# Two feed-forward layers behind chunked attention: other buffers and another order where the second layer begins, and one sum reordered in the last pass

## The chip, the cores and the metric

The kernel runs on one core of one Trainium2 chip. The metric is device time in microseconds (us); one number is the median of three runs. The engines are called as in the profile: PE is TensorE (matmul), PEld its weight load, DVE is VectorE, ACT is ScalarE, POOL is GpSimd, and SP is SyncE, whose one queue (SPq) issues every transfer of this kernel in program order.

## What is computed

```python
def reference(**kwargs):                      # batch 8, heads 8, seq 576, head_dim 64
    attn_out = _attn_ref(q, k, v)             # softmax attention inside chunks of 64
    x = attn_out.transpose(0, 2, 1, 3).reshape(B * S, H * D)      # 4608 tokens x 512
    g = x @ w_gate                            # 512 -> 1536
    x = silu(g) * (x @ w_val) @ w_out         # layer 1: 1536 -> 512
    h = x @ w_in                              # 512 -> 2048
    return h * sigmoid(1.702 * h) @ w_out2    # layer 2: 2048 -> 512
```

Everything is float32. Each number is split into a high part that PE multiplies exactly (fp32r) and a low remainder, and a product is three matmuls (high*high, high*low, low*high: lines 249, 250 and 251).

## The kernel before

**Tiling.** The 4608 tokens are nine blocks of 512 (`b` = 0 to 8). The program makes four passes over the blocks, two for layer 1 (`p` = 0, 1) and two for layer 2 (`p` = 2, 3). A pass holds a part of the hidden width in SBUF; in layer 2 a pass has two groups of four times 128 hidden columns. Products of 2x2 blocks are made with seven multiplications in place of eight (Strassen and Winograd), so everything comes in sevens, under the labels "1" to "7".

**One layer-2 group** is `group_gated` (line 632). Its seven input products (`product`, 12 matmuls of 128 columns by 256 tokens each) go through PSUM. As a rule all seven share one bank, `ga`: some labels add on top of the former one, others start the bank anew, and between two products ACT or DVE reads the bank out (`follow`, line 660, into the tiles `u` and `c`). Such a product cannot start before the bank was read. Where `early` is set, labels "2", "3" and "4" have the banks `gb`, `s` and `a` for themselves, and the order is "1263745". From the four finished quarters, `gate` (line 647) makes h * sigmoid(1.702 h): a Sigmoid on ACT (line 651 in the profile) and a multiply on DVE. The four results stand in one tile of the ring `xr`, which has one buffer only. DVE then adds them up to the seven combinations, and `parts` (line 656) splits each into high (a cast on ACT) and low (a subtraction on DVE or POOL). The homes of the parts are the buffers of `HOMES` (line 629): `hh`, `hl`, `h`, `q`, `k`, `v`, `xt`.

**The second product** of a group is 14 `last_product`s (line 714), two per label in the order "1245673", each 6 matmuls. They add over the two groups of a pass into seven half banks: "1" and "2" in `ya`, "4" and "5" in `yb`, "6", "7", "3" in `gb`, `s`, `a` (`o_banks`, line 726). After the second group `o_sum` (line 732) reads them out; in pass 2 it stores partial sums to DRAM, in pass 3 it adds the stored ones and writes the output. The last products of one group are interleaved with the input products of the next (`put`, line 874).

**Where the layers meet.** At the end of pass 1 `block_sum` (line 795) finishes the layer-1 output of a block in a tile of `xr`; `x_to_dram` (line 556) forms seven token combinations (`token_combos`: four subtractions, three of them into the three buffers of `xt`), splits each by ACT plus DVE or POOL, and stores both halves to DRAM, where layer 2 loads them. For the last block the seven splits take seven different pairs of buffers.

**Weights.** The weights of the next pass are converted during a pass (`group_to_dram`, line 403): loads into the ring `raw`, four ACT instructions and four DVE instructions per tile (lines 328 to 337), sums `st`, a cast and a subtraction on POOL into `ws`, a store. Each pair of tiles is a job; `spread` (line 848) gives the eight jobs of pass 2 a due time each. A job takes two tiles of the ring `t` and two loads of two half tiles, so four Sigmoid-sized ACT instructions of line 328.

**What sets the order.** All instructions are recorded as `op`s with an estimated cost, a priority (`prio`, a due time in us; lower is first) and their dependences. `Program.emit` (line 99) then writes each engine's queue: it always takes the op that can start earliest by these estimates, and the priority decides only between ops that can start within 0.1 us (DVE) or 0.3 us (the others) of each other. For layer 2, hand-overs between ACT, DVE and POOL are planned at 1.0 us (`prog.slack`). The order is fixed before the kernel runs.

**Names used below.** G0 and G1 are the two groups of pass 2, block 0, so the first two groups of layer 2; H0 is the first group of block 1. Before, only G0 has `early`.

```python
alone = {"2": "gb", "3": "s", "4": "a"} if early else {}
z = ring["ga"].new([P, 2, HT])
bank = {label: ring[alone[label]].new([P, 2, HT]) if label in alone else z for label in ORDER[2]}
for i, label in enumerate("1263745" if early else ORDER[2]):
```

Of the kernel before, what the change touches and what calls it, by code (L numbers as in the profile page):

```python
# [13 lines left out]
ALU = mybir.AluOpType  # L14
# [4 lines left out]
P = 128  # L19
# [122 lines left out]
def attention_two_moe_kernel(ctx: ExitStack, tc: tile.TileContext, q, k, v, wg, wv, wo, wi, wo2, out):  # L142
# [36 lines left out]
    HT = BT // 2  # L179
    NB = NT // BT  # L180
# [77 lines left out]
    for layer, nf, per in ((1, NF1, 6), (2, NF2, 8)):  # L258
        for f0 in range(0, nf, per):
            gs = []  # L260
            for j in range(0, per, 2 * layer):
                g = Group()
# [199 lines left out]
    xr = {}  # L462
# [93 lines left out]
    def x_to_dram(xb, b, prio):  # L556
        for n, (m, src, cut) in enumerate(token_combos(xb, prio)):
            i = ORDER[2].index(m)
            pairs = ["qk", "ve"] if b < NB - 1 else ["qk", "ve", "tt", ("raw", "raw"), ("ws", "ws"), "hh", "te"]
            hi, lo = [ring[t].new([P, 2, HT], F32R) for t in pairs[n % len(pairs)]]  # L560
            split(hi, lo, src, 512, prio + n, "pool" if b < NB - 1 else ("dve", "pool")[n % 2], cut)
            for c, s in enumerate((hi, lo)):
                store(x_dram[1][:, b, i, c * 512:(c + 1) * 512], Buf(lambda s=s: s.ap.rearrange("p a t -> p (a t)"), None, None, s), [xd[1][b][i].part(None)], prio + n + 2)
# [65 lines left out]
    HOMES = {"1": ("hh", "hl"), "2": ("hh", "hl"), "4": ("hh", "hl"), "5": ("h", "h"), "6": ("q", "k"), "7": ("v", "xt"),  # L629
             "3": ("xt", "xt")}  # L630

    def group_gated(g, xs, at, put, early):


        s1, u2, u3 = [ring["u"].new([P, 2, HT]) for _ in range(3)]
        made = {}
        hs = []

        quarters = []

        def quarter():
            if not quarters:
                c = ring["c"].new([P, 2, 2, HT])
                quarters.extend(c.part(lambda ap, k=k: ap[:, k]) for k in range(2))
            return quarters.pop(0)

        def gate(c, k, prio):
            if not hs:
                hs.append(ring["xr"].new([P, 4, 2, HT]))
            h = hs[0].part(lambda ap: ap[:, k])  # L650
            op("act", act_us(512), lambda: nc.scalar.activation(out=h.ap, in_=c.ap, func=AF.Sigmoid, scale=1.702),  # L651
               [c], [h], prio, "sig")
            tt(h, h, c, ALU.mult, 512, prio)
            return h

        def parts(label, src, prio, eng="dve"):
            made[label] = [ring[t].new([P, 2, HT], F32R) for t in HOMES[label]]
            split(*made[label], src, 512, prio, eng)

        def follow(label, prio):  # L660
            m = bank[label]
            if label == "1":
                copy(s1, m, 512, prio, near=0.3)
            elif label == "6":
                copy(u2, m, 512, prio, near=0.3)
            elif label == "7":
                copy(u3, m, 512, prio, near=0.3)
                tt(u2, u2, u3, ALU.subtract, 512, prio, "pool")
            elif label == "5":
                c = quarter()  # L670
                copy(c, m, 512, prio, near=0.3)
                tt(u2, u2, c, ALU.add, 512, prio, "pool")
                a["22"] = gate(c, 3, prio + 1)
                parts("4", a["22"], prio + 3, "pool")
            elif label == "2":
                c = quarter()
                tt(c, s1, m, ALU.add, 512, prio, near=0.3)
                a["11"] = gate(c, 0, prio + 1)
                parts("1", a["11"], prio + 2)
            elif label == "4":  # L680
                c = quarter()
                tt(c, u3, m, ALU.subtract, 512, prio, near=0.3)
                a["12"] = gate(c, 1, prio + 1)
                parts("2", a["12"], prio + 3)
            else:
                c = quarter()
                tt(c, u2, m, ALU.add, 512, prio, near=0.3)
                a["21"] = gate(c, 2, prio + 1)

        a = {}  # L690
# [4 lines that stand above are left out]
            n = ORDER[2].index(label)  # L695
            product(bank[label], W[g][n], xs[n], label in "675", at(i), 0.25)
            if label != "3" or not early:
                follow(label, at(i))
            if i == 6:
                if early:  # L700
                    follow("3", at(i))
                prio = at(i)
                tt(a["22"], a["21"], a["22"], ALU.add, 512, prio + 1)
                parts("5", a["22"], prio + 2)
                tt(a["21"], a["11"], a["21"], ALU.subtract, 512, prio + 2)
                tt(a["11"], a["22"], a["11"], ALU.subtract, 512, prio + 2)
                parts("6", a["11"], prio + 3)
                parts("7", a["21"], prio + 4)
                tt(a["12"], a["12"], a["11"], ALU.subtract, 512, prio + 4)
                parts("3", a["12"], prio + 5)  # L710
            put(i)
        return made
# [19 lines left out]
    def o_sum(p, b, label, banks, kept, prio):  # L732

        final = p == NPASS - 1

        def part_of(k, tag):

            t = ring[tag].new([P, 2, 256])
            if final:
                load(t.part(lambda ap: ap.rearrange("p a c -> p (a c)")), o_dram[:, b, k], prio - 14, [od2[b, k]])  # L740
            return t

        def out_quarter(k, t):
            if final:
                t0 = b * BT + (k // 2) * HT
                dst = out[t0:t0 + HT, k % 2 * 256:k % 2 * 256 + 256].rearrange("(t p) c -> p t c", p=P)
                store(dst, t, [], prio)
            else:
                od2[b, k] = Buf(None)
                store(o_dram[:, b, k], Buf(lambda: t.ap.rearrange("p a c -> p (a c)"), None, None, t), [od2[b, k]], prio)  # L750

        m = banks[label]
        if label == "1":
            kept["s"] = ring["e"].new([P, 2, 256])
            copy(kept["s"], m, 512, prio)
        elif label == "2":
            c = part_of(0, "yv")
            if final:
                tt(c, c, kept["s"], ALU.add, 512, prio, "pool")
                tt(c, c, m, ALU.add, 512, prio)  # L760
            else:
                tt(c, kept["s"], m, ALU.add, 512, prio)
            out_quarter(0, c)
        elif label == "6":
            tt(kept["s"], kept["s"], m, ALU.add, 512, prio)
        elif label == "7":
            u2, u3 = kept["s"], ring["e"].new([P, 2, 256])
            tt(u3, u2, m, ALU.add, 512, prio)
            c = part_of(3, "yv")
            if final:  # L770
                tt(c, c, u3, ALU.add, 512, prio, "pool")
                tt(c, c, banks["5"], ALU.add, 512, prio)
            else:
                tt(c, u3, banks["5"], ALU.add, 512, prio)
            out_quarter(3, c)
            c = part_of(2, "t") if final else u3
            if final:
                tt(c, c, u3, ALU.add, 512, prio, "pool")
            tt(u2, u2, banks["5"], ALU.add, 512, prio)
            tt(c, c, banks["4"], ALU.subtract, 512, prio)  # L780
            out_quarter(2, c)
            if final:
                kept["c"] = part_of(1, "t")
                tt(kept["c"], kept["c"], u2, ALU.add, 512, prio, "pool")
        elif label == "3":
            u4 = kept["c" if final else "s"]
            tt(u4, u4, m, ALU.add, 512, prio)
            out_quarter(1, u4)
# [6 lines left out]
    def block_sum(p, b, ys, e, prio):  # L795
# [10 lines left out]
            xr[b] = ring["xr"].new([P, KD, BT])  # L806
        tt(xr[b].part(lambda ap: ap[:, e]), s, ys[e], ALU.add, 512, prio)
        if e == KD - 1:
            x_to_dram(xr.pop(b), b, prio + 3)


    op("pool", 0.6, lambda: make_identity(nc, ident.ap), [], [ident], -99)
# [14 lines left out]
    early = [((g.name, var, i), g.pairs[var][i]) for g in gs0[:2] for var in range(2) for i in range(2)]  # L827
# [3 lines left out]
    for u in range(UPB):  # L831
        bufs = None
        if u:
            ve = ring["c"].new([P, 2, 512])
# [13 lines left out]
    def spread(p):  # L848

        if p + 1 >= NPASS:  # L850
            return []
        jobs = [j for g in passes[p + 1][1] for j in group_to_dram(g, 0)]
        a = start[p][0] + (100 if p == 0 else 10)
        z = start[p + 1][0] - 60
        return [(a + (z - a) * i / len(jobs), j) for i, j in enumerate(jobs)]

# [6 lines left out]
    for p, (layer, gs) in enumerate(passes):  # L863
        jobs = spread(p)
        for b in range(NB):
            t = start[p][b]
            xs = X.pop((p, b))
            for j, g in enumerate(gs):
# [30 lines left out]
                            pend.append(fn)  # L899
                else:  # L900
                    prog.slack = 1.0
                    parts = group_gated(g, xs, at, put, after_first)
                    if j == 0:
                        banks, kept = {}, {}
                    ws = {}
# [84 lines left out]
```

## Time and profile before

| | us |
|---|---|
| median of 3 runs (lowest, highest) | 1790.44 (1789.31, 1791.83) |
| the profiled execution, its own time | 1790.32 |
| its span, first to last instruction | 1788.5 |
| PE busy in it | 1711.5 (96%) |
| DVE / ACT / POOL busy | 1310.8 / 876.9 / 761.6 |

The profiled execution stands 1.8 us above its span (start and end of the program) and 0.1 us below the median. Pass 2 begins on PE at about 1014 us of the span, pass 3 at about 1398 us. Busy time of PE has to be read with the count of matmuls beside it: at half clock a matmul counts as busy for longer, and matmuls overlap.

### The profile page before, as it was taken

What the parts mean: (1) busy time and instruction counts of PE and PEld (TensorE: products, weight loads), DVE (VectorE), ACT (ScalarE), POOL (GpSimd) and SP (SyncE); (2) the same over time, 40 slices, a digit from 0 to 9 for tenths busy, and PEclk for the clock granted to TensorE, in tenths of its full rate; (3) what the DMA queues carried; (4) which work ended last, traced back from release to release, by engine and by line L of the source; (5) the groups of instructions that cost most, each with busy time, mean ns of one, the idle gap of its engine ahead of it and who ended that gap; (6) DMA issues with size and microseconds to landing.
All of it is one profiled execution on the core that took longest, in us unless ns stands there. A gap on an engine that the chain in (4) does not pass through costs nothing.

```text
span 1788.5 us, 36703 instructions
## 1 busy us (share of the span) xinstructions
PE 1711.5 (96%) x14392; PEld 1623.6 (91%) x14392; DVE 1310.8 (73%) x1884; ACT 876.9 (49%) x1534; POOL 761.6 (43%) x762
## 2 busy tenths in 40 slices
PE   6779999999999999999999978999999999999997
PEld 6769988989899999999999968999999999999997
DVE  6887788778876477655555679888877677777777
ACT  6766665666563344333333354555544444444442
POOL 5664455455632145412222247556651233334333
PEclk8889999999999999999999998999999999999999
DMA  7468887788768989877778988788888977666664
GB/s 254 167 217 271 270 298 239 253 297 285 245 236 329 339 288 314 284 260 247 251 246 304 367 323 280 266 277 286 290 279 304 360 262 237 232 213 224 225 220 152
DMA packets 187325, 477.93 MB, mean 267 GB/s; under 512 B 20112, under 2 KB 47760, under 8 KB 187152
## 3 DMA queue, kind: packets, MB, share of 16 engines
q1 hardware_dynamic: 187152, 475.58, 77.6%
q8 instruction: 114, 1.87, 0.4%
q14 instruction: 59, 0.48, 0.1%
HBM read 334.46 MB, written 141.03 MB: 266 GB/s over the span
## 4 chain that ended last, share of the span: by engine, by line
PE 75%; DVE 15%; issue 3%; DMA 1%; ACT 1%; POOL 0%; POOLq 0%; SPq 0%; DVEq 0%; ACTq 0%
PE ga L249 9%; PE ga L251 9%; PE ga L250 9%; PE yb L249 4%; PE ya L250 4%; PE ya L251 4%; PE ya L249 4%; PE yb L251 4%; PE yb L250 4%; PE gb L249 4%; PE gb L251 4%; PE gb L250 4%; DVE xr L242 3%; PE s L249 2%; PE s L251 2%
## 5 line engine op out<-in xcount | busy, mean ns | idle before, releaser
L249 PE MATMUL ga<-x,w 128*128 128x256 f32 x1652 | 477.1, 289 | 28.8 <-DVE c L242 12.1
L250 PE MATMUL ga<-x,w 128*128 128x256 f32 x1652 | 468.6, 284 | 3.0 <-DVE x L242 3.0
L251 PE MATMUL ga<-x,w 128*128 128x256 f32 x1652 | 468.7, 284 | 0.1
L249 PEld LDWEIGHTS ga<-x,w 128*128 128x128 f32 x1652 | 314.8, 191 | 43.4 <-DVE c L242 18.2
L250 PEld LDWEIGHTS ga<-x,w 128*128 128x128 f32 x1652 | 314.9, 191 | 7.6 <-DVE x L242 3.3
L251 PEld LDWEIGHTS ga<-x,w 128*128 128x128 f32 x1652 | 314.8, 191 | 0.3 <-POOL w L242 0.3
L233 ACT COPY u<-ga 128x512 f32<-128x512 f32 x231 | 135.1, 585 | 254.6 <-PE ga L251 249.8
L242 DVE TENSOR_TENSOR c<-u,ga 128x512 f32<-128x512 f32 x146 | 99.8, 684 | 138.4 <-PE ga L251 137.1
L242 DVE TENSOR_TENSOR h<-h,c 128x512 f32<-128x512 f32 x216 | 170.6, 807 | 10.0 <-ACT h L613 8.4
L651 ACT ACTIVATE xr<-c 128x512 f32<-128x512 f32 x144 | 90.0, 631 | 162.4 <-DVE c L242 118.1
L249 PE MATMUL gb<-x,w 128*128 128x256 f32 x496 | 143.0, 288 | 2.4 <-DVE c L242 2.4
L251 PE MATMUL gb<-x,w 128*128 128x256 f32 x496 | 141.4, 285 | 0.0
L250 PE MATMUL gb<-x,w 128*128 128x256 f32 x496 | 141.1, 284 | 0.0
L242 POOL TENSOR_TENSOR u<-u 128x512 f32<-128x512 f32 x36 | 53.7, 1492 | 191.7 <-ACT u L233 191.7
L242 DVE TENSOR_TENSOR c<-u,gb 128x512 f32<-128x512 f32 x124 | 84.6, 682 | 67.4 <-ACT u L233 42.3
L613 ACT ACTIVATE h<-c 128x512 f32<-128x512 f32 x108 | 68.1, 633 | 120.5 <-DVE c L242 120.2
L242 DVE TENSOR_TENSOR xr<-xr,c 128x512 f32<-128x512 f32 x144 | 115.7, 809 | 14.2 <-ACT xr L651 14.2
L242 DVE TENSOR_TENSOR xr<-xr 128x512 f32<-128x512 f32 x144 | 118.1, 820 | 1.4
L235 POOL CAST ws<-t 128x256 fp32r<-128x256 f32 x78 | 45.3, 581 | 172.3 <-DMA od_b<-ws 81.3
L242 POOL TENSOR_TENSOR k<-xr,q 128x512 fp32r<-128x512 f32 x24 | 42.3, 1762 | 158.3 <-DVE xt L242 63.9
L249 PEld LDWEIGHTS gb<-x,w 128*128 128x128 f32 x496 | 95.2, 192 | 5.6 <-DVE c L242 3.0
L235 POOL CAST ws<-st 128x256 fp32r<-128x256 f32 x88 | 48.4, 549 | 121.2 <-DMA od_b<-ws 54.0
(239 smaller groups left out, 5179.2 us busy)
## 6 DMA issues: line engine op xcount, KB each, us to landing
x<-x_dram SPq DMA_DIRECT2D x189, 512.0 KB, 5.5
o<-od_b SPq DMA_DIRECT2D x126, 512.0 KB, 4.5
o<-od_a SPq DMA_DIRECT2D x102, 512.0 KB, 5.2
x_dram<-x SPq DMA_DIRECT2D x63, 512.0 KB, 4.7
wd_b<-ws SPq DMA_DIRECT2D x56, 256.0 KB, 4.8
od_b<-ws SPq DMA_DIRECT2D x56, 256.0 KB, 5.2
w<-wd_b SPq DMA_DIRECT2D x28, 512.0 KB, 6.8
raw<-in_moe_w_out SPq DMA_DIRECT2D x56, 255.8 KB, 5.1
```

What stands on the lines that cost most here:

```text
L233: op("act", act_us(n), lambda: nc.scalar.copy(out=dst.ap, in_=cut(src.ap)), [src], [dst], prio, near=near)
L235: op("pool", pool_us(0.6 * n), lambda: nc.gpsimd.tensor_copy(dst.ap, cut(src.ap)), [src], [dst], prio)
L242: lambda: e.tensor_tensor(out=dst.ap, in0=of_a(a.ap), in1=of_b(b.ap), op=by), [a, b], [dst], prio, near=near)
L249: nc.tensor.matmul(o, ah, bh, start=first, stop=False, **kind)
L250: nc.tensor.matmul(o, ah, bl, start=False, stop=False, **kind)
L251: nc.tensor.matmul(o, al, bh, start=False, stop=last, **kind)
L613: op("act", act_us(512), lambda h=h, i=i: nc.scalar.activation(out=h.ap, in_=of(0)(c[i].ap), func=AF.Sigmoid), [c[i]], [h], prio, "sig")
L651: op("act", act_us(512), lambda: nc.scalar.activation(out=h.ap, in_=c.ap, func=AF.Sigmoid, scale=1.702), [c], [h], prio, "sig")
```

## The change

1. `x_to_dram` for the last block splits through two pairs of buffers, (`raw`, `raw`) and (`ws`, `ws`), in turn, in place of seven pairs; a pair is free again when both its stores have landed. Its sums and splits get a priority 5 us later.
2. G0's gates (`apart`) write to three tiles of `t` and one of `e` in place of the one tile of `xr`.
3. G1 gets `early`: the banks `gb`, `s`, `a` and the order "1263745".
4. The conversion jobs of pass 2 are due from 70 us after the start of the pass, before 10; their last due time stays.
5. `o_sum` of pass 3: before, POOL added quarter 2's partial sum to u3 and DVE then subtracted bank "4"; now DVE subtracts bank "4" from u3 in place first, and POOL adds the result to the stored sum last. In pass 2 the same instructions come in the same order.

```diff
@@ x_to_dram
-            pairs = ["qk", "ve"] if b < NB - 1 else ["qk", "ve", "tt", ("raw", "raw"), ("ws", "ws"), "hh", "te"]
+            pairs = ["qk", "ve"] if b < NB - 1 else [("raw", "raw"), ("ws", "ws")]
@@ group_gated
-    def group_gated(g, xs, at, put, early):
+    def group_gated(g, xs, at, put, early, apart):
         def gate(c, k, prio):
-            if not hs:
-                hs.append(ring["xr"].new([P, 4, 2, HT]))
-            h = hs[0].part(lambda ap: ap[:, k])
+            if apart:
+                h = ring["ttte"[k]].new([P, 2, HT])
+            else:
+                if not hs:
+                    hs.append(ring["xr"].new([P, 4, 2, HT]))
+                h = hs[0].part(lambda ap: ap[:, k])
@@ o_sum
             out_quarter(3, c)
+            tt(u2, u2, banks["5"], ALU.add, 512, prio)
+            tt(u3, u3, banks["4"], ALU.subtract, 512, prio)
             c = part_of(2, "t") if final else u3
             if final:
                 tt(c, c, u3, ALU.add, 512, prio, "pool")
-            tt(u2, u2, banks["5"], ALU.add, 512, prio)
-            tt(c, c, banks["4"], ALU.subtract, 512, prio)
             out_quarter(2, c)
@@ block_sum
-            x_to_dram(xr.pop(b), b, prio + 3)
+            x_to_dram(xr.pop(b), b, prio + (3 if b < NB - 1 else 8))
@@ spread
         a = start[p][0] + (100 if p == 0 else 10)
+        if p == 2:
+            a += 60
@@ the loop over groups
-                    parts = group_gated(g, xs, at, put, after_first)
+                    parts = group_gated(g, xs, at, put, after_first or p == 2 and b == 0, after_first)
```

## Rows read from the trace of the kernel before

**Rows 1.** The page, part 1: busy us, share of the span, instructions.

```profile
PE 1711.5 (96%) x14392; PEld 1623.6 (91%) x14392; DVE 1310.8 (73%) x1884; ACT 876.9 (49%) x1534; POOL 761.6 (43%) x762
```

**Rows 2.** Windows: length, busy us (instructions) of PE, PEld, DVE, ACT, POOL; PEclk, DMA share, GB/s.

```profile
1030.00:1074.00 44.00, 32.00 (x237) 29.97 (x237) 33.27 (x43) 23.80 (x45) 20.31 (x20) 0.96 0.89 319
1074.00:1095.00 21.00, 16.35 (x105) 15.65 (x104) 19.12 (x26) 9.11 (x17) 12.36 (x14) 0.76 0.70 228
...
1100.00:1300.00 200.00, 196.09 (x1631) 194.18 (x1631) 175.69 (x245) 109.28 (x198) 125.05 (x135) 1.00 0.85 287
1350.00:1400.00 50.00, 50.00 (x423) 50.00 (x423) 33.37 (x51) 22.50 (x38) 9.07 (x7) 1.00 0.88 317
```

**Rows 3.** Waits of PE from 1020 to 1110: us in total, times, longest us.

```profile
PE ga L249 <- DVE c L242: 8.2, 4, 5.5
PE yb L251 <- DVE h L242: 3.6, 1, 3.6
PE ga L249 <- ACT u L233: 3.4, 5, 0.7
```

**Rows 4.** Timeline of PE: start us, us, what [idle before <- releaser].

```profile
1048.58 0.58 PE L249 MATMUL ga<-x,w 128*128 128x256 f32 x1 [5.46 <-DVE c L242]
...
1074.00 0.28 PE L249 MATMUL ya<-o,hh 128*128 128x256 f32 x1
...
1078.32 0.28 PE L249 MATMUL ga<-x,w 128*128 128x256 f32 x1
...
1083.77 0.58 PE L251 MATMUL yb<-o,h 128*128 128x256 f32 x1 [3.61 <-DVE h L242]
```

**Rows 5.** Timeline of DVE where the layers meet.

```profile
1035.21 0.68 DVE L242 TENSOR_TENSOR xt<-xt,xr 128x512 f32<-128x512 f32 x1
...
1042.92 1.75 DVE L242 TENSOR_TENSOR e<-xr,t 128x512 fp32r<-128x512 f32 x1
...
1047.84 0.68 DVE L242 TENSOR_TENSOR c<-u,ga 128x512 f32<-128x512 f32 x1
```

**Rows 6.** Timeline of ACT: the four Sigmoids of G0 and of G1.

```profile
1044.77 2.19 ACT L651 ACTIVATE xr<-c 128x512 f32<-128x512 f32 x4 [3.86 <-DVE e L242]
...
1064.77 2.18 ACT L651 ACTIVATE xr<-c 128x512 f32<-128x512 f32 x4
```

**Rows 7.** Timeline of DVE in G1's parts: a conversion, and the low half of part "5".

```profile
1075.01 1.52 DVE L333 SCALAR_TENSOR_TENSOR t<-t,raw 128x256 int32<-128x256 f32 x1
...
1082.84 0.88 DVE L242 TENSOR_TENSOR h<-xr,h 128x512 fp32r<-128x512 f32 x1
```

**Rows 8.** DMA issues from 1000 to 1100: count, KB each, median us to landing.

```profile
w<-od_b SPq DMA_DIRECT2D x7, 512.0 KB, 9.6
...
x_dram<-raw SPq DMA_DIRECT2D x2, 256.0 KB, 4.6
```

**Rows 9.** Waits of PE from 1400 to 1760.

```profile
PE yb L249 <- DVE t L242: 3.9, 8, 0.5
```

**Rows 10.** Timeline of PE in pass 3, second block.

```profile
1470.96 0.38 PE L249 MATMUL yb<-w,hh 128*128 128x256 f32 x1 [0.49 <-DVE t L242]
...
1472.76 0.39 PE L249 MATMUL ga<-x,w 128*128 128x256 f32 x1
```

**Rows 11.** Timeline of DVE, same stretch.

```profile
1463.44 1.77 DVE L242 TENSOR_TENSOR h<-xr,h 128x512 fp32r<-128x512 f32 x1
...
1468.53 0.68 DVE L242 TENSOR_TENSOR yv<-yv,yb 128x512 f32<-128x512 f32 x1
...
1470.23 0.68 DVE L242 TENSOR_TENSOR t<-t,yb 128x512 f32<-128x512 f32 x1
...
1472.03 0.68 DVE L242 TENSOR_TENSOR c<-u,ga 128x512 f32<-128x512 f32 x1
```

**Rows 12.** Timeline of POOL, same stretch.

```profile
1462.93 3.43 POOL L242 TENSOR_TENSOR t<-t,e 128x512 f32<-128x512 f32 x2
...
1468.39 1.37 POOL L242 TENSOR_TENSOR u<-u,c 128x512 f32<-128x512 f32 x1 [0.33 <-ACT c L233]
```

**Rows 13.** Timeline of DVE: the last compute instruction of the kernel.

```profile
1784.79 0.69 DVE L242 TENSOR_TENSOR t<-t,a 128x512 f32<-128x512 f32 x1 [0.54 <-POOL t L242]
```

## The prediction

> **What bounds the kernel now.** PE, nearly everywhere: 96% of the span [rows 1]. So only stretches in which PE does less than it can are worth a change, and I look for them first by windows, then by PE's waits, then by the timeline of whoever ends the wait. The undisturbed rate stands in the window 1350 to 1400: 423 matmuls in 50 us, 0.118 us each [rows 2]; an input product (12 matmuls) is then 1.42 us, a last product 0.71 us. Against that rate the window 1030 to 1074 does 237 matmuls, 28.0 us of work in 44 us, so 16.0 us are lost; 1074 to 1095 does 105, 12.4 us in 21, so 8.6 us are lost [rows 2]. Together 24.6 us at the place where the layers meet, the place that edits 1 to 4 touch. Part is waiting: 8.2 us for DVE's `c`, 3.4 for ACT's `u` (both mean: the one bank `ga` was not yet read out), 3.6 for the low half `h` [rows 3]. Part is the clock: its mean granted share is 0.76 in the second window [rows 2], and the first matmul after each long wait takes 0.58 us where one after a short wait takes 0.38 [rows 4, 10].
>
> Why the long wait of 5.46 us [rows 4]: DVE's `c` came at 1047.84 [rows 5], because it needs a buffer that G0's gates still read; these gates started at 1044.77, released by the last layer-1 split at 1042.92 [rows 5, 6], since both use the one buffer of `xr`. Why the second, 3.61 us [rows 4]: DVE is behind, a conversion op taking 1.52 us among G1's parts [rows 7].
>
> In pass 3 a smaller wait returns in eight blocks: 0.49 us for `t<-t,yb` [rows 9, 10].
>
> **The change, part by part.**
>
> *G0's gates leave `xr`, its parts leave no shared buffers (edits 1, 2).* The quarters are then gated as they come, some 15 us before 1044.77 for the first ones. Instructions are the same in number; nothing is added on any engine. The last products of G0 become ready before PE has finished G1's input products, but for "7" and "3", whose `xt` buffers wait for splits.
>
> *G1 in separate banks (edit 3).* G1's five short waits for `u` and `c`, 0.7 to 0.9 us each [rows 3], and the one of 5.46 [rows 4] go, with about 1.5 us (an estimate from the 0.58) of slow matmuls after the long one: some 11 us of the 16.0. This is no gain by itself: PE only comes sooner to its next wait. The banks are free, since `o_banks` takes `gb` for label "6" only after the eight products of the labels "1", "2", "4" and "5".
>
> *What is late next: the serial splits (edit 1).* The seven splits run through two pairs of buffers, so four rounds, and a round lasts until the stores have landed. A cast is about 0.6 us (a Sigmoid of the same size, four in 2.19 [rows 6]), the subtraction 0.7 to 1.75 [rows 5], issue to landing 4.6 [rows 8], hand-overs about 0.5: 7 us. The sums ended at 1035.9 before [rows 5]; now G0's gates and sums come on DVE at the same time with the better priority, some eight instructions of 0.6 us, so I take 1041. Three rounds and a last cast and subtraction: 1041 + 21 + 2 = 1064. Only then is `xr` free, and G1's gates need it. They started at 1064.77 before [rows 6]: so G1's gates come no sooner. PE has 28.4 us of work from 1030 until it needs them (seven products of G1, twelve last products of G0, seven products of H0), so it waits about 6 us here.
>
> *The conversion put behind (edit 4).* After G1's gates the first last product of G1 (`ya<-o`) came at 1074.00 [rows 4], 9.2 us later, because the conversion had the better priority on DVE and POOL. Gate, multiply, cast and subtraction with hand-overs are about 7 us without it: 1072. H0's last input product came at 1078.32 [rows 4]; now it is done before. So at 1074 PE is ahead by 2.0 + 1.4 = 3.4 us. From 1074 on, the loss of 8.6 us goes as far as it was the conversion's; I leave 2.6 us, for the clock after the new idle time and some waits. Sum for the place: 3.4 + 6.0 = 9.4 us. Bounds: only the 3.4, or all but 6 of the 24.6, so 18.6.
>
> The jobs come again later: eight of them at 28.6 us from each other, 36.1 before (the planned 359 us of a pass, less 130 or 70, by eight). In 1100 to 1300 PE did 1631 matmuls where 1692 were possible, 7.2 us lost [rows 2], with about six of the jobs: 1.2 us a job. Two more fall there: 2.4 us. Bounds: nothing, and 5 (closer jobs hide less well).
>
> SP's queue: the x_dram stores are the same fourteen, issued later, each behind its split; loads queued behind them (x for H0, weights for G1) are issued as soon as a buffer is free, some products ahead of their use, and that covers it. If the cover goes, see the third rival.
>
> *The sum in pass 3 (edit 5).* Per block PE loses 0.49 us at `yb`, then starts the following `ga` product late as well: from `yb` at 1470.96 to `ga` at 1472.76 are 1.80 us where 1.42 would do [rows 10]. With two restarts (first matmuls of 0.38 and 0.39 us [rows 10], 0.28 without a wait [rows 4]) this is 0.49 + 0.38 + 0.2, about 1.1 us per block. The second delay has another cause: DVE reads `c` only at 1472.03 [rows 11], as it is behind. So freeing `yb` alone gives nothing; DVE must come sooner to `c`. It was held up at 1463 to 1468, where instructions with two SBUF operands take 1.77 us beside POOL, those with a PSUM operand 0.68 [rows 11]; POOL had `t<-t,e` twice there, 3.43 us [rows 12]. One of these two now comes after DVE's subtraction, so after `u<-u,c` at 1468.39 [rows 12]. By the planner's rule the subtraction from u3 takes the slot of `t<-t,yb` at 1470.23; the rest of DVE's order stays. POOL then rests twice in the crowded stretch, DVE gains two waits of 1.1 us, and the moved addition costs one again, at `xt` behind the subtraction, with 0.3 us of gaps lost: 0.8 us. Eight blocks: 6.4 us. Bounds: nothing, and 8 x 1.1 = 8.8.
>
> At the very end POOL has the same three additions in another order ahead of DVE's last instruction [rows 13]: between 0.7 us gained and 0.7 lost; I take nothing.
>
> **Sum.** 9.4 - 2.4 + 6.4 = 13.4 us. From the profiled execution's 1790.3 that is 1776.9; the median stands 0.1 higher: 1777.
>
> **The rivals.**
>
> *Pass 3 gains nothing* (1783.4, chance 0.16). DVE stays behind by as much, since the moved addition catches another instruction for each one that it lets go. The Trainium skill, page "SBUF — State Buffer", section "Who interferes with whom", says that a VectorE instruction with two SBUF inputs and a GpSimd one that reads SBUF exclude each other for the whole instruction, the later one waiting. The 1.77 against 0.68 us agrees with it [rows 11]. Against this rival: in the new place two of the four DVE instructions have a PSUM operand and run on.
>
> *The place where the layers meet gains nothing beyond what is given back* (1786, chance 0.13). For it: G1's gates wait for `xr` as before, and the 6 us of idle time lower the clock. Then 2.4 us are lost to the conversion and 6.4 gained in pass 3.
>
> *Slower* (1795, chance 0.07): each round through two pairs takes 13 us instead of 7, because DMA is full here (share 0.89 [rows 2]; weight loads landed after 9.6 us [rows 8]) and the stores stand in SP's queue behind loads. Then `xr` is free at 1041 + 39 + 2 = 1082, G1's last products start at 1089, 15 us later than before; 1.4 (H0's last product) and 4.7 (later waits saved) come back, 2.4 are paid for the conversion, 6.4 are gained in pass 3: 15 - 1.4 - 4.7 + 2.4 - 6.4 = 4.9 us slower. It decides from rounds of 12 us on.
>
> *The due time does nothing* (1783, chance 0.08): the priority only orders ops that are ready together, and with POOL and ACT idle the conversion starts as soon as `raw` is free, at about 1069. Then the 6.0 us after 1074 stay lost.
>
> **How the numbers follow.** My forecast, both places gaining, has 0.56; its own range is 1770 to 1783. With the rivals the range is 1768 to 1788; what it leaves out is the slow case and a tenth on the fast side. About 0.2%, 3.6 us, is what a measurement of this kernel can tell from no change: faster means under 1786.9. Faster: 0.56 + 0.16 + 0.08 and half of 0.13, so 0.86; the same 0.07; slower 0.07.
>
> **What would show it.** In the profile after: no waits of `ga` for `c` and `u` between 1029 and 1040; G0's Sigmoids from about 1020 on, writing `t` and `e`; G1's Sigmoids at 1062 to 1067 and `ya<-o` within 8 us of them; between them one idle time of PE of about 6 us. In pass 3 no wait for `t<-t,yb`, and every block 0.8 us shorter than now. I am wrong if G1's Sigmoids come after 1070, if conversions run beside G1's parts again, or if the eight waits of pass 3 are merely at `ga` instead.

## The result, and the profile after

| | before | after |
|---|---|---|
| median, us (lowest to highest) | 1791.13 (1789.31 to 1792.23) | 1775.33 (1773.35 to 1778.04) |
| ratio to before, 95% interval | | 0.9911 [0.9894, 0.9927] |
| profiled execution, its own time | 1790.32 | 1773.35 |

The change makes the kernel 15.8 us faster by the medians, where 13.4 were forecast. The total came out inside the range, but its terms did not: two gains were larger than forecast and one cost was more than four times as large. That the total came so close is in part luck.

To compare terms I use one measure throughout, **PE's lost time**: the time between the starts of successive matmuls beyond 0.1185 us (0.236 for those with 512 columns), summed over a stretch of the profiled execution; excesses of 0.01 us or less are left out. It is finer than the medians: executions of one kernel differ by some 8 us here, and part of that arises ahead of the change (G0's first Sigmoid came at 1017.00 us after, and at 1021.33 in the first run with casts on ACT, with the same work up to there).

| lost, us | 1025 to 1100, the place | 1100 to 1375, the conversion | pass 3 | the end |
|---|---|---|---|---|
| before | 24.8 | 6.8 | 9.05 | 5.3 |
| after | 7.9 | 17.4 | 0 | 4.6 |

That is 16.9 - 10.6 + 9.05 + 0.7 = 16.1 us of the 17.0 between the two profiled executions. The 0.7 us at the end can't be told from chance: the runs below that have edit 5 lose between 4.6 and 6.5 us there.

Busy time, and the windows that answer to [rows 1] and [rows 2]:

```profile
PE 1702.8 (96%) x14392; PEld 1617.6 (91%) x14392; DVE 1307.8 (74%) x1884; ACT 878.3 (50%) x1534; POOL 765.7 (43%) x762
```

```profile
1030.00:1074.00 44.00, 38.73 (x315) 37.50 (x314) 29.30 (x46) 21.81 (x40) 14.94 (x13) 1.00 0.86 315
1074.00:1095.00 21.00, 20.27 (x171) 20.07 (x170) 18.57 (x29) 11.50 (x22) 6.16 (x5) 1.00 0.95 340
1100.00:1300.00 200.00, 189.30 (x1556) 186.88 (x1556) 179.36 (x244) 107.99 (x196) 133.52 (x140) 0.99 0.85 284
```

Look at the counts: 315 matmuls where 237 stood, 171 where 105 stood, PEclk 1.00 in both windows where it was 0.96 and 0.76; then 1556 where 1631 stood. The share of busy time, 96% in both, shows none of this.

PE's waits from 1020 to 1110 after [rows 3]: the long wait for `c` and the one for `h` are gone, the short ones are not.

```profile
PE ga L249 <- ACT u L233: 3.5, 5, 0.7
PE ga L249 <- DVE c L242: 2.5, 2, 1.7
PE ya L249 <- ACT e L233: 0.7, 1, 0.7
```

PE's longest idle time at the place, and the first last product of G1 [rows 4], which starts without a wait:

```profile
1062.47 0.39 PE L249 MATMUL ga<-x,w 128*128 128x256 f32 x1 [1.66 <-DVE c L242]
...
1063.99 0.28 PE L249 MATMUL ya<-o,hh 128*128 128x256 f32 x1
```

ACT's timeline after [rows 6]: G0's four Sigmoids (the line is 654 now), the four casts into `raw` of the last splits, and G1's Sigmoids. G0's come 14 to 28 us sooner than the 1044.77 of before; the rounds of a pair last 7.6, 5.2 and 5.2 us.

```profile
1017.00 0.63 ACT L654 ACTIVATE t<-c 128x512 f32<-128x512 f32 x1
...
1030.76 0.63 ACT L654 ACTIVATE t<-c 128x512 f32<-128x512 f32 x1
...
1036.94 0.62 ACT L233 CAST raw<-xr 128x512 fp32r<-128x512 f32 x1
...
1044.52 0.62 ACT L233 CAST raw<-xt 128x512 fp32r<-128x512 f32 x1
...
1049.74 0.62 ACT L233 CAST raw<-xr 128x512 fp32r<-128x512 f32 x1
...
1054.92 0.62 ACT L233 CAST raw<-xr 128x512 fp32r<-128x512 f32 x1 [0.29 <-DMA x_dram<-raw]
...
1058.65 2.20 ACT L654 ACTIVATE xr<-c 128x512 f32<-128x512 f32 x4 [3.12 <-DVE raw L242]
```

DVE's timeline after: the end of the sums, the last subtraction from `xr` (which frees it), the four multiplies of G1's gates and the `c` behind them that PE waits for, the first conversion [rows 7], and pass 3 [rows 11].

```profile
1038.71 0.68 DVE L242 TENSOR_TENSOR xt<-xt,xr 128x512 f32<-128x512 f32 x1
...
1057.93 0.69 DVE L242 TENSOR_TENSOR raw<-xr,raw 128x512 fp32r<-128x512 f32 x1 [0.29 <-DMA x_dram<-raw]
...
1059.32 2.50 DVE L242 TENSOR_TENSOR xr<-xr,c 128x512 f32<-128x512 f32 x4
1061.73 0.68 DVE L242 TENSOR_TENSOR c<-u,ga 128x512 f32<-128x512 f32 x1
...
1065.24 0.41 DVE L333 SCALAR_TENSOR_TENSOR t<-t,raw 128x256 int32<-128x256 f32 x1
...
1455.90 1.77 DVE L242 TENSOR_TENSOR h<-xr,h 128x512 fp32r<-128x512 f32 x1
1457.59 0.68 DVE L242 TENSOR_TENSOR xr<-xr 128x512 f32<-128x512 f32 x1
...
1460.50 0.68 DVE L242 TENSOR_TENSOR k<-xr,q 128x512 fp32r<-128x512 f32 x1
...
1461.70 0.68 DVE L242 TENSOR_TENSOR xt<-xr,xt 128x512 fp32r<-128x512 f32 x1
1462.30 0.68 DVE L242 TENSOR_TENSOR t<-t,a 128x512 f32<-128x512 f32 x1
1463.04 0.69 DVE L242 TENSOR_TENSOR c<-u,ga 128x512 f32<-128x512 f32 x1
1463.64 1.69 DVE L242 TENSOR_TENSOR xr<-xr,c 128x512 f32<-128x512 f32 x1
```

POOL in the same stretch of pass 3 [rows 12]: the pair of 3.43 us is one addition and, 6.5 us after it began, another.

```profile
1455.39 1.73 POOL L242 TENSOR_TENSOR t<-t,e 128x512 f32<-128x512 f32 x1
1457.97 1.45 POOL L242 TENSOR_TENSOR u<-u 128x512 f32<-128x512 f32 x1 [0.85 <-ACT u L233]
1461.85 1.68 POOL L242 TENSOR_TENSOR t<-t,e 128x512 f32<-128x512 f32 x1 [2.42 <-DVE e L242]
```

Of the eight waits for `t<-t,yb` [rows 9] none is left, and no other took their place: in the window 1395 to 1740, which holds seven of the eight, PE does 2906 matmuls after, 2839 before.

The new loss lies in the conversion. Waits of PE from 1100 to 1375, in the kernel before and then after:

```profile
PE ga L249 <- DVE c L242: 3.5, 4, 1.5
```

```profile
PE ga L249 <- DVE c L242: 9.8, 6, 3.0
PE ga L249 <- ACT u L233: 1.0, 3, 0.4
PE ya L249 <- ACT e L233: 0.7, 1, 0.7
```

### The profile page after: what moved, and what is told of

It reads as the page before. It is cut to its first block, busy times and chain, and to the rows that moved or that the text cites. A ratio compares the mean times of both kernels' runs of the same rounds, so it can differ in the third digit from the quotient of the medians.

```text
span 1771.6 us, 36678 instructions
## 1 busy us (share of the span) xinstructions
PE 1702.8 (96%) x14392; PEld 1617.6 (91%) x14392; DVE 1307.8 (74%) x1884; ACT 878.3 (50%) x1534; POOL 765.7 (43%) x762
## 4 chain that ended last, share of the span: by engine, by line
PE 76%; DVE 11%; DMA 5%; issue 2%; POOL 1%; ACT 1%; SPq 0%; POOLq 0%; ACTq 0%; DVEq 0%
PE ga L249 9%; PE ga L251 9%; PE ga L250 9%; PE yb L249 4%; PE ya L250 4%; PE ya L251 4%; PE ya L249 4%; PE yb L251 4%; PE yb L250 4%; PE gb L249 4%; PE gb L251 4%; PE gb L250 4%; DVE xr L242 2%; PE s L249 2%; PE s L250 2%
## 5 line engine op out<-in xcount | busy, mean ns | idle before, releaser
L242 DVE TENSOR_TENSOR h<-h,c 128x512 f32<-128x512 f32 x216 | 170.6, 807 | 12.6 <-ACT h L613 10.9
L242 DVE TENSOR_TENSOR xr<-xr,c 128x512 f32<-128x512 f32 x140 | 128.4, 924 | 12.9 <-ACT xr L654 12.7
L235 POOL CAST ws<-t 128x256 fp32r<-128x256 f32 x78 | 50.6, 649 | 162.2 <-DVE h L242 65.0
L242 DVE TENSOR_TENSOR xr<-xr 128x512 f32<-128x512 f32 x140 | 111.2, 794 | 1.4
```

The lines of the kernel that those rows point to most:

```text
L235: op("pool", pool_us(0.6 * n), lambda: nc.gpsimd.tensor_copy(dst.ap, cut(src.ap)), [src], [dst], prio)
L242: lambda: e.tensor_tensor(out=dst.ap, in0=of_a(a.ap), in1=of_b(b.ap), op=by), [a, b], [dst], prio, near=near)
```

## The experiments

Two questions stood open: which edit the gains belong to, and what makes the conversion cost 17.4 us. Losses below are given as place / conversion stretch; before has 24.8 / 6.8, sum 31.6, and after 7.9 / 17.4, sum 25.3. They are the sums of gaps in one execution each, so a difference of 1 us in them says little. The 5 us later priority in edit 1 was never undone by itself.

### The sum of pass 3 alone

The kernel before with edit 5 only.

```diff
+            tt(u2, u2, banks["5"], ALU.add, 512, prio)
+            tt(u3, u3, banks["4"], ALU.subtract, 512, prio)
             c = part_of(2, "t") if final else u3
...
-            tt(u2, u2, banks["5"], ALU.add, 512, prio)
-            tt(c, c, banks["4"], ALU.subtract, 512, prio)
```

> The kernel before with the reordered sum of pass 3 alone. Theory: the sum is worth what the stalls of pass 3 were, 8 blocks of 1.13 us between matmul starts, all of them gone in the changed kernel: 9.0 us, so 1782 beside 1791, and a window of 50 us in pass 3 holds 423 matmuls instead of 413. Rival, as predicted blind: DVE still comes late to c, 0.8 us a block, 6.4 us, and 0.3 us a block stay as a late ga product. Second rival: the gain in pass 3 hangs on what the other edits changed upstream; then the waits at yb stay and the time is 1791.

Measured: 1782.88 us (1780.44 to 1784.03), ratio 0.9948 [0.9929, 0.9967]. Lost 24.9 / 6.5, as before (up to pass 3 the two kernels are the same, so these sums repeat within 0.3 us); nothing in pass 3, where its window 1395 to 1740 has the 2906 matmuls of after. The ratio is 9.3 us of before's 1790.32. So edit 5 is worth the whole 9.05 us by itself and needs none of the others.

### Without the later due times

```diff
-        if p == 2:
-            a += 60
```

> The changed kernel without the 60 us by which the conversion jobs of pass 2 are due later. The changed kernel lost 7.9 us of PE where the layers meet (24.6 before) and 17 us beside the conversions from 1095 to 1350 (6.8 before). Theory A: the closer due times (28.6 us instead of 36.1) make the later loss; without the delay it falls back to about 7 us, while conversion ops come among G1's parts again with the better priority and cost some 6 us there: about 1771, and the delay is a net cost of 4 us. Rival B: the delay is what the gain where the layers meet rests on, and the later loss has another cause: 17 us stay and 10 us or more come back at the place: 1785 or more.

Measured: 1780.47 us (1775.88 to 1784.35), ratio 0.9935 [0.9911, 0.996]. Lost 14.3 / 14.0, sum 28.3. The delay saves 6.4 us at the place and costs 3.4 later: it moves the loss more than it removes it. Even without it the conversion stretch loses 14.0, twice the 6.8 of before, with the same 24 of DVE's conversions (line 333) in it, so neither the delay nor the number of jobs is the main cause there. By the times alone this run can't be told from after: the intervals overlap. Theory A was right about the place and wrong about the later loss, rival B the other way round.

### G1 in the one bank

```diff
-                    parts = group_gated(g, xs, at, put, after_first or p == 2 and b == 0, after_first)
+                    parts = group_gated(g, xs, at, put, after_first, after_first)
```

> The changed kernel with one bank (ga) for G1 again, label order 1675243. Theory: with G0's gates early, G0's last products fill the time between two products on ga, so the separate banks are worth only the short waits that are left: 0 to 3 us slower than the changed kernel. Rival: the banks are a condition of the gain, since product after product on ga has to be read out (0.7 to 0.9 us each, and longer while DVE is full): 6 us or more slower.

Measured: 1777.99 us (1774.7 to 1783.82), ratio 0.9916 [0.9893, 0.994]. Lost 17.4 / 12.6, sum 30.0 against 25.3 after. By the times alone it can't be told from after; by the gaps G1's banks save 9.5 us at the place, and half of it is lost again later. The profiled execution is the slowest of the four (1783.82 us), so these gaps are the least certain ones here.

### Seven pairs for the last splits

```diff
-            pairs = ["qk", "ve"] if b < NB - 1 else [("raw", "raw"), ("ws", "ws")]
+            pairs = ["qk", "ve"] if b < NB - 1 else ["qk", "ve", "tt", ("raw", "raw"), ("ws", "ws"), "hh", "te"]
```

> The changed kernel with the seven pairs of buffers for the last seven splits. Theory: the pairs take t, e, hh, hl, q, k, v and h, which G0's gates and parts now want early; by the order in which the buffers are handed out the splits come first, so G0's gates wait for the stores of t and e, and the place where the layers meet loses nearly what it lost before: 12 us or more slower than the changed kernel, PE idle for some us around 1045. Rival: the serial splits are the price of the change (G1's gates wait for xr through them), and with seven pairs xr is free 10 us sooner: 2 us or more faster.

Measured: 1782.09 us (1777.96 to 1782.37), ratio 0.994 [0.992, 0.996]. The later priority of edit 1 stays. Lost 17.9 / 14.4, sum 32.3: with seven pairs the other edits gain nothing at the place and in the conversion together. The run is 7 us slower than after, not the 12 or more expected. ACT's timeline shows why: a Sigmoid of G0 into `e` waits until a split's store from `e` has landed.

```profile
1047.15 0.63 ACT L654 ACTIVATE e<-c 128x512 f32<-128x512 f32 x1 [5.74 <-DMA x_dram<-e]
```

And PE waits for the read-out that stands behind it in ACT's queue:

```profile
1051.42 0.58 PE L249 MATMUL ga<-x,w 128*128 128x256 f32 x1 [15.41 <-ACT c L233]
```

### G0's gates back in `xr`

```diff
-                    parts = group_gated(g, xs, at, put, after_first or p == 2 and b == 0, after_first)
+                    parts = group_gated(g, xs, at, put, after_first or p == 2 and b == 0, False)
```

> The kernel after, but G0's gates write to the one tile of xr again (edit 2 undone alone). Theory (edit 2 is the condition for edit 1: with two buffer pairs the last layer-1 split leaves xr only at about 1058 us, and G0's gates would stand behind it): G0's four Sigmoids start after 1055 instead of 1017 to 1031, PE loses 25 to 45 us between 1025 and 1100 instead of 7.9, the median is 1790 to 1805, so the rest of the change is worth nothing without it. Rival (the place was gained by G1's own banks, edit 3, and PE has enough input products to go on with): PE loses under 15 us there, and the median stays within 1774 to 1783.

Measured: 1788.94 us (1786.13 to 1791.4), ratio 0.998 [0.9968, 0.9992]. Lost 32.6 / 3.9, sum 36.5. The four Sigmoids start at 1060.62, all in one, and PE stands idle longer than ever in this case:

```profile
1064.89 0.58 PE L249 MATMUL ga<-x,w 128*128 128x256 f32 x1 [22.89 <-ACT c L233]
```

So edit 2 is the condition of edit 1, as edit 1 is of edit 2 (the run before). The median lies 1 us under what the theory gave, since the conversion stretch lost 3.9 and not 17.4, though the jobs are the same (26 of DVE's conversions of line 333 in the stretch, 694 ns each; 28 of 712 after) and DVE is as busy there (239.2 us, after 239.8, before 230.4). A reading of this: PE had been held back 32.6 us, so DVE was no longer behind it when the conversion came. The two stretches are not independent; only their sum can be set against another version's.

### Conversion jobs 36 us from each other

After, but the last due time moved 60 us back as well, so that the due times are no closer together than before.

```diff
-        z = start[p + 1][0] - 60
+        z = start[p + 1][0] - (60 if p != 2 else 0)
```

> The changed kernel with the last due time of the conversion jobs of pass 2 moved back by 60 us as well, so that the eight jobs are 36 us from each other as before. Theory A (closer jobs make the later loss): the 17.4 us lost between 1100 and 1375 fall to some 8, 8 us faster than the changed kernel. Rival B (a job costs PE about 2 us wherever it falls, since POOL's conversion instructions hold up DVE): 14 to 17 us stay, spread over a longer stretch, within 3 us of the changed kernel. The run without the delay, where the spacing was 36 us too and 14.0 us were lost, speaks for B.

Measured: 1775.05 us (1773.64 to 1778.75), ratio 0.9905 [0.9885, 0.9925]. Lost 7.8 / 16.0, so the closer due times explain 1.4 us of the 10.6 at most. But the edit hardly moved the jobs: DVE's 32 conversions of line 333 start from 1067.4 to 1323.5 here, from 1065.2 to 1315.6 after and from 1053.6 to 1298.7 before, so over 256, 250 and 245 us. The due times came closer, the jobs did not. That is the stronger reason why the spacing, which the prediction gave for its upper bound, is not the cause.

### A third pair for the splits

```diff
-            pairs = ["qk", "ve"] if b < NB - 1 else [("raw", "raw"), ("ws", "ws")]
+            pairs = ["qk", "ve"] if b < NB - 1 else [("raw", "raw"), ("ws", "ws"), ("yv", "yv")]
```

> The changed kernel with a third pair of buffers (yv, yv) for the last seven splits, so three rounds instead of four. In the changed kernel xr came free at 1058.6 and PE lost 7.9 us between 1025 and 1100. Theory (the serial splits are what is late there): xr free 5 us sooner, G1's Sigmoids at about 1053, G0's parts 7 and 3 sooner too, the loss falls to about 4 us: 3 to 4 us faster, unless the conversion stretch takes it back. Rival (the serial splits are covered by PE's other work): G1's Sigmoids earlier, but the loss stays at 7 to 8 us.

Measured: 1776.42 us (1772.95 to 1778.67), ratio 0.9907 [0.9883, 0.9932]. Lost 6.9 / 16.3. A miss: the casts into `raw` came at 1040.48, 1048.06 and 1058.49, fewer rounds but longer ones, and the time is that of after. G1's Sigmoids came at 1060.61, 40.2 us behind G0's first one, where after has 41.7: three rounds saved 1.5 us and not 5. So whether sooner splits would help PE stays open.

### POOL fills in place of converting

After, with the order of every queue kept, but POOL's conversion instructions of pass 2 replaced by fills with a constant, which read nothing. The weights of pass 3 are left out by this.

```diff
+        elif eng == "pool" and fill[0]:
+            op("pool", pool_us(0.6 * n), lambda: nc.gpsimd.memset(bits(dst.ap), 0.01), [src], [dst], prio)
...
+        if eng == "pool" and fill[0]:
+            op(eng, pool_us(n), lambda: nc.gpsimd.memset(bits(dst.ap), 0.01), [a, b], [dst], prio, near=near)
+            return
```

> The changed kernel, every instruction in the same order, but in the conversion of pass 2 POOL fills its outputs with a constant instead of casting, adding and subtracting: the weights of pass 3 are left out. Theory (POOL's reads of SBUF hold up DVE's instructions with two SBUF operands, and this is the later loss): DVE's instructions return to 0.7 us and the 17.4 us lost between 1100 and 1375 fall under 5: 1762. Rival (DVE has too many instructions in this stretch, whatever POOL does): 12 us or more stay lost.

Measured, one run: 1760.2 us; lost 8.5 / 4.0. And the same filling in the kernel before:

> The same constant filling in the kernel before. Theory: between 1074 and 1100 the wait of 3.6 us for h and the slow clock after it go, since both came from DVE held up by POOL's conversion: some 8 of the 24.8 us lost between 1025 and 1100, and most of the 6.8 us after it. Rival: the wait for h came from the conversion's instructions on DVE itself, and 3 us or more of it stay.

Measured, one run: 1780.84 us; lost 21.0 / 2.1. There the wait for `h` [rows 3] went, but a wait of 2.9 us for ACT's `u` took part of its place: 3.8 us came back at the place, not the 8 expected, and 4.7 of the 6.8 behind it.

DVE's groups from 1100 to 1375 show what happened. The rows are DVE's sums of two SBUF operands, and its read-out of a PSUM bank. Before:

```profile
L242 DVE TENSOR_TENSOR xr<-xr 128x512 f32<-128x512 f32 x53 | 40.6, 767 | 0.4
L242 DVE TENSOR_TENSOR c<-u,ga 128x512 f32<-128x512 f32 x41 | 28.1, 684 | 34.9 <-PE ga L251 33.6 <-POOL hl L242 1.2
```

After:

```profile
L242 DVE TENSOR_TENSOR xr<-xr 128x512 f32<-128x512 f32 x55 | 48.3, 878 | 0.3
L242 DVE TENSOR_TENSOR c<-u,ga 128x512 f32<-128x512 f32 x39 | 26.6, 683 | 26.4 <-PE ga L251 26.1 <-issue 0.2
```

After, with the fills:

```profile
L248 DVE TENSOR_TENSOR xr<-xr 128x512 f32<-128x512 f32 x55 | 38.8, 705 | 0.3
L248 DVE TENSOR_TENSOR c<-u,ga 128x512 f32<-128x512 f32 x41 | 28.1, 686 | 44.2 <-PE ga L257 44.1
```

The sums fall from 878 to 705 ns, the read-out stays at 683 and 686. And DVE, which waited 26.1 us for PE's products in this stretch, now waits 44.1: it is ahead of PE again. The Trainium skill, page "SBUF — State Buffer", section "Who interferes with whom", says that a VectorE instruction with two SBUF inputs contends with a GpSimd instruction that reads SBUF, and not with one that only writes it. The trace agrees, with these four numbers. The fills are also shorter than what they replace (312 ns, where POOL's subtractions take 854 to 890), so a rival is that POOL is merely done sooner. Two things in the traces speak against it. Sorted by what POOL does at the same time, the 29 sums of after beside which POOL does nothing take 683 ns in the mean and the 24 beside a conversion instruction 1063; in the run with fills the 10 beside fills alone take 685. And from 1100 to 1375 of after no wait of PE or of DVE is ended by POOL, and ACT waits for POOL 2.5 us in all.

### The casts on ACT

If POOL's reading is the cause, a version with less of it should beat both kernels. The first one is the run with due times 36 us apart, with the jobs' casts on ACT; a second has every other cast on ACT and the jobs due 30 us later in place of 60.

```diff
-                    split(hi, lo, src, 256, prio + j, "pool", cut, "pool")
+                    split(hi, lo, src, 256, prio + j, "pool", cut, "act" if g in passes[3][1] else "pool")
...
-        z = start[p + 1][0] - 60
+        z = start[p + 1][0] - (60 if p != 2 else 0)
```

> The kernel after, with the eight conversion jobs of pass 2 spread as in the run with 36 us between them, and the casts of these jobs on ACT instead of POOL (as many instructions, same reads). Theory (POOL's conversion instructions that read SBUF hold up DVE's instructions with two SBUF operands): POOL then has one instruction per tile in place of two, so PE's loss from 1100 to 1375 falls from 16.0 us to 6 to 12, DVE's conversion instruction of line 333 takes clearly less than 612 ns in the mean, and the median comes to 1767 to 1773. Rival 1 (what is late is DVE's own work of the jobs, whatever POOL does): 14 to 17 us stay lost there and the median is 1774 to 1778. Rival 2 (the casts are now ahead of the read-outs of PSUM in ACT's queue): waits of ga for ACT's u of together more than 4 us appear from 1100 to 1375 and the median is 1774 to 1782.

Measured: 1767.8 us (1764.33 to 1771.4), ratio 0.9863 [0.9843, 0.9884]; lost 7.4 / 11.0. Its windows 1030 to 1095 and 1100 to 1375:

```profile
1030.00:1095.00 65.00, 59.44 (x481) 57.74 (x480) 48.79 (x73) 33.48 (x61) 19.95 (x15) 1.00 0.91 331
1100.00:1375.00 275.00, 269.09 (x2225) 266.29 (x2224) 233.17 (x333) 162.68 (x318) 136.41 (x124) 0.99 0.87 288
```

and the sums of DVE there:

```profile
L242 DVE TENSOR_TENSOR xr<-xr 128x512 f32<-128x512 f32 x56 | 44.8, 800 | 0.3
```

ACT does 318 instructions where 258 stood in the run with POOL's casts, and of PE's waits there 0.7 us are for its `u`, 2.0 us for ACT's copies in all, so ACT had the room. The sums take 800 ns, 888 with POOL's casts. One of the theory's numbers failed: DVE's conversion of line 333 takes 671 ns in this stretch, hardly less than the 700 with POOL's casts. The quotient of the two ratios, 0.9863 to 0.9911, is 0.9952 [0.9925, 0.9978]: this version beats the kernel after, by some 8 us. The casts alone are to be read against the run with the same due times: 16.0 to 11.0 us in the stretch, 1775.05 to 1767.8 us in the median.

The second:

```diff
-                    split(hi, lo, src, 256, prio + j, "pool", cut, "pool")
+                    split(hi, lo, src, 256, prio + j, "pool", cut, "act" if g in passes[3][1] and j % 2 else "pool")
...
-            a += 60
+            a += 30
```

> The kernel after, with the jobs of pass 2 due 30 us later instead of 60 and every second cast of theirs on ACT instead of POOL. Theory (POOL's reading of SBUF, and when the jobs start, set the loss): PE's loss from 1100 to 1375 falls from 17.4 to 9 to 14 us; between 1025 and 1100 it lies between the 7.9 of the kernel after and the 14.3 without the delay; the median is 1770 to 1776. Rival (only DVE's own share of the jobs counts): the sum of the two stretches stays at 25 us or more, and the median at 1775 to 1780.

Measured: 1770.36 us (1769.24 to 1773.65), ratio 0.9881 [0.9864, 0.9897]; lost 12.2 / 9.5, sum 21.7 where the full move has 18.4. The loss at the place lies between those of the two due times, as expected. Two things were changed at once, so what each is worth isn't separated.

## Why the prediction was right

The forecast, faster by 13.4 us through both places, held: 1777.0 was given, 1775.33 measured. The two places and the mechanisms of the gains were right; that the total came so close is luck. By its steps:

**What is late next at the place.** Right in kind: G0's gates went to 1017 to 1031 as forecast (from about 1020 on), `xr` became free behind serial splits, and G1's gates followed at once. The size was off. The step was "three rounds and a last cast and subtraction: 1041 + 21 + 2 = 1064"; measured it was 1036.94 + 18.0 + 3.7 = 1058.6. The first cast did not wait for the sums, which ended at 1039.4; I had added the 4.6 us of [rows 8] and one estimate for every hand-over, and two of three rounds took 5.2; the last cast and subtraction took longer. About 1.4 us of it are no gain, since this execution came to the place that much sooner (the last two additions into `xr` began at 1030.69 us, before at 1032.08). Then from the Sigmoids to `ya<-o` it was 5.3 us (1058.65 to 1063.99), 9.2 before, about 7 forecast.

The idle time "of about 6 us" between the two did not come. It did not fit its own step either: work until 1058.4 and `ya<-o` at 1072 leave over 13 us, and the 6 counted only up to the gates. (The sum went by the 1072.) In the trace `ya<-o` starts without a wait; the 1.66 us just before are a wait of an H0 product for DVE's `c`, which stood behind the four multiplies of G1's gates (2.50 us from 1059.32). The clock never fell, and the place gained 16.9 us, not 9.4. Between my bounds of 3.4 and 18.6 the value lay near the upper one.

**G1's banks.** The waits of `ga` for `c` and `u` between 1029 and 1040 went as forecast. Eight short ones, 6.7 us with `ya`'s, come from 1047 on, at the groups behind, whose products have `ga` alone; the 1.66 us are one of them.

**The conversion.** This term failed. "1.2 us a job", times two jobs, took the price of a job for a constant; the stretch lost 10.6 us more, twice my upper bound of 5, with one job more in it and not two (28 of DVE's conversions, 24 before). The runs show in its place: closer due times are worth 1.4 us at most and the whole delay 3.4; POOL's conversion, read against fills, costs the kernel after 17.4 - 4.0 = 13.4 us here, and the kernel before 6.8 - 2.1 = 4.7 here and 24.8 - 21.0 = 3.8 at the place. So the price of a job depends on the schedule around it. Why it is higher after is argued and not shown, and two readings stand. One is DVE's lag: before, PE was held up at the place, and DVE went into the conversion with a lead; after, PE is hardly held up, and more of the time that POOL costs DVE comes out as waits at `ga`. The run with G0's gates in `xr` speaks for it (32.6 / 3.9, with DVE as busy as after). The other is that POOL's instructions hold DVE's up for longer in the new order: the sums take 767 ns before, 749 in that run, 878 after. No run set either by itself.

**Pass 3.** 9.05 us, forecast 6.4: the mechanism was right, and the step "the moved addition costs one again, at `xt` behind the subtraction" was not. `xt<-xr,xt` at 1461.70 takes 0.68 us; it starts before POOL's addition at 1461.85. The DVE instruction that pays is `xr<-xr,c` at 1463.64, 1.69 us, behind the `c` of 1463.04, where PE does not wait for it. What DVE gained ahead of `c` was one wait of 1.1 us (a sum, 1.78 to 0.68) and one of 0.5 (`k<-xr,q`, 1.18 to 0.68), not two of 1.1. All of the loss went, 1.13 us per block, a little more than the upper bound of 8.8. The two instructions before:

```profile
1465.14 1.78 DVE L242 TENSOR_TENSOR xr<-xr 128x512 f32<-128x512 f32 x1
...
1469.13 1.18 DVE L242 TENSOR_TENSOR k<-xr,q 128x512 fp32r<-128x512 f32 x1
```

**The end.** Nothing was forecast. The 0.7 us gained are no more than runs differ by there.

**The rivals.** "Pass 3 gains nothing" fell by the 2906 matmuls. "The place gains nothing" fell by G1's Sigmoids at 1058.65 and the clock of 1.00, "slower" by the rounds of 5.2 to 7.6 us, where 12 were needed. "The due time does nothing" was half right: one job did start as soon as `raw` was free, at 1065.24, beside G1's parts, which the prediction had named as a sign of being wrong; but no wait of PE for a part of G1 followed. The total came out right by luck: 7.5 us too little gain at the place and 8.2 too little cost after it nearly cancelled, and 2.65 too little in pass 3 was small.

## What to carry to other kernels

When a change lets PE wait less, work beside it can cost more than it did: here PE lost 6.8 us beside the conversion jobs before and 17.4 beside the same jobs after. So price background work in the schedule that the change makes, not in the one that it ends. Where DVE is nearly full, look whether POOL's instructions that read SBUF can be done on ACT, or come when DVE has only PSUM operands to read; here the first was worth 5 us in the stretch and some 7 in the median, the second 9. And edits that lean on each other are tried together: undone one at a time, the place and the conversion lost 3.0 (due times), 4.7 (banks), 7.0 (pairs) and 11.2 us (gates), far more than the 6.3 that all four bring together.

## What was not expected of the hardware

Moving the casts of the conversion from POOL to ACT (ACT has 60 instructions more from 1100 to 1375) shortened DVE's sums of two SBUF operands from 888 to 800 ns in the mean, and yet left DVE's conversions with two SBUF operands nearly as they were (700 and 671 ns). POOL's own remaining subtractions grew slightly, from 925 to 955 and from 950 to 1019 ns. Beside no POOL instruction a conversion of line 333 takes 417 ns (POOL's casts) and 419 (ACT's), beside one 761 and 835; with the casts on ACT 17 of the 28 still meet one, 23 with POOL's casts. Why those last longer isn't shown.

After an idle time of 15.41 or 22.89 us PE's first matmul takes 0.58 us, those behind it start 0.21 us apart (PE's lower level, 1.2 GHz, where 0.118 us is the rate at 2.4), and the granted clock of the window 1025 to 1100 is 0.89 and 0.82; after 1.66 us the first matmul takes 0.39, and the clock stays at 1.00.
